# An attention and expert kernel on one core: GpSimd's place behind VectorE, and the seed of the last ranking

## The chip, the core and the metric

The kernel runs on one core of a Trainium2 chip. The metric is device time in microseconds (us) of one execution; a stated time is the median of its runs. TensorE (PE) multiplies matrices, VectorE (DVE), ScalarE (ACT) and GpSimd (POOL) work elementwise, SyncE (SP) issues transfers.

## The reference

Four batches, eight heads, 768 tokens, 64 dimensions a head: 32 heads in all. Each query and key gets a bucket from the signs of six projections, and a query attends only to keys of its own bucket. The heads' outputs are laid side by side as x, and in each batch the 128 tokens with the highest gate score go through a two-layer expert.

```python
def _attn_ref(q, k, v, proj):
    ...
    mask = q_bucket[:, :, :, None] == k_bucket[:, :, None, :]
    scores = scale * np.matmul(q, k.transpose(0, 1, 3, 2))
    scores = np.where(mask, scores, -1000000000.0)
    scores = scores - np.max(scores, axis=-1, keepdims=True)
    attn = np.exp(scores)
    attn = attn / (np.sum(attn, axis=-1, keepdims=True) + 1e-09)
    return np.matmul(attn, v)

def _moe_ref(x, w_gate, w1, w2, capacity):
    scores = np.einsum('bsd,d->bs', x, w_gate)
    out = x.copy()
    for b in range(B):
        top_idx = np.argpartition(-scores[b], capacity)[:capacity]
        xe = x[b, top_idx]
        h = np.maximum(xe @ w1, 0.0)
        ye = h @ w2
        g = 1.0 / (1.0 + np.exp(-scores[b, top_idx]))
        out[b, top_idx] = x[b, top_idx] + g[:, None] * ye
    return out
```

## The kernel before, in words

**Work and order.** The kernel cuts all its work into some 2,500 small steps (a function with its arguments), records them in a list, and then calls them in the order of a table of numbers, `ORDER`. Entry k calls step k; a negative entry resumes one of eight generators (-1 is `weights`, -2 to -4 are `choose` for batches 0 to 2, -5 is `rank_last` for the last batch). The calls run under a manual schedule, so each engine's instructions stand in the order in which the table calls them. An engine works through its own list in order and waits on semaphores only where data or buffers need it.

**A head.** For each head h and each of its six blocks of 128 queries, `max_unit` multiplies the block with the keys in two halves (L671, two of four rotating PSUM banks), `max_relu` (ACT, L679) reads the first half and frees its bank, `max_red` (DVE, L688, tile mj) combines it with the second half into a row maximum in M, and frees that bank. M is turned and written back into a row of A by way of a transfer, so that the scores come out already reduced by the maximum. `st_unit` (PE, L722 and L726) makes the transposed scores and `st_exp` (ACT, L740 and L742) their exponentials P in fp32. For a precise product, P is used as its high half (read straight out of the fp32 words) and a rest R = P minus that half. `r_chunk` makes R: for one chunk of 128 keys on DVE (L757, 128x768), or for a pair of chunks on GpSimd (L760, 128x1536). GpSimd has the middle pair in even heads and the two outer pairs in odd heads. `av` (PE, L776) multiplies P and R with V, three matmuls a block. Then `recip` and `norm` (DVE, L786 to L798) divide into x.

**Other work of the two engines.** DVE also makes low halves: of the projected inputs (L502), of V (L556), of key differences (L661) and of signs (L487), each an instruction with two inputs in SBUF. `score` (L813, tile jks) multiplies x with the gate weights and sums, also two SBUF inputs. GpSimd makes the low halves of the expert's weights (L837, 128x512) as `weights` is resumed.

**How GpSimd is ordered against DVE.** `mine(i)` remembers a DVE instruction with two SBUF inputs, the latest one in `ORDER`; `turn(i)` makes a GpSimd instruction wait by semaphore for the one remembered at that point. So which DVE instruction a GpSimd one waits for is set by where its entry stands in `ORDER`. A GpSimd instruction is free to start while later DVE instructions with two SBUF inputs run. L813 is not remembered before the change (except where another function wraps it).

**The last batch.** After the last head, `rank_last` broadcasts the scores along rows with twelve fp32 matmul passes (L1143, tiles bp) that ACT copies to sbc (L1149), DVE compares them (L859), PE counts into rp (L866), DVE turns the counts into a rank (L1167) and six `pick` instructions (L874) make a 0/1 selection out of it, which PE multiplies with x (L1177). The PSUM tiles here rotate through a pool of three buffers, which the keep-warm matmuls (L311, tile wq) take from too. Between them PE runs the expert of batch 2 (L995, L1019).

Of the kernel before, what the change touches and what calls it, by code (L numbers as in the profile page):

```python
# [20 lines left out]
P = 128  # L21
# [222 lines left out]
def body(ctx, tc, qk, v, pj, wg, w1, w2, cst, out):  # L244
# [114 lines left out]
    def mine(i):  # L359
        st["port"] = i  # L360
# [441 lines left out]
    def score(b, part, d0, d1, t0, t1):  # L802

        if ("sc", b, part) not in st:
            st["sc", b, part] = sb.tile([P, NC], F32, tag=f"sc{part}", name=f"sc{b}_{part}", bufs=1)
        need(*(("nd", b * H + d // D) for d in range(d0, d1, D)))
        x, sc = st["x", b], st["sc", b, part]
        if part:
            need(*(("scd", b, 0, t) for t in range(t0, t1)))
        for t in range(t0, t1):  # L810
            st["scd", b, part, t] = True
            jk = sb.tile([P, 384], BF16, tag="jks", name=f"jks{b}_{part}_{t}", bufs=2)
            nc.vector.tensor_tensor_reduce(  # L813
                out=jk[:, : d1 - d0], in0=x[:, t, d0:d1], in1=wgt[:, d0:d1],
                op0=ALU.mult, op1=ALU.add, scale=1.0,
                scalar=st["sc", b, part - 1][:, t : t + 1] if part else 0.0,
                accum_out=sc[:, t : t + 1],
            )
# [45 lines left out]
    def count(i, cm, rp):  # L864
        for j in range(i, NC):
            nc.tensor.matmul(  # L866
                rp[:, j : j + 1], cm[:, j], oneb[:, 0:1], start=(i == j == NC - 1), stop=(i == 0),
                skip_group_check=True,
            )
# [259 lines left out]
    def rank_last(b):  # L1129
# [23 lines left out]
        rp = st_bank(f"rp{b}")  # L1153
        yield
        cnt = sb.tile([P, NC], F32, tag="cnt", name=f"cnt{b}", bufs=1)
        cms = {}
        for i in range(NC - 1, -1, -1):
# [3 lines left out]
            if i < NC - 1:  # L1161
                count(i + 1, cms[i + 1], rp)
                yield
        count(0, cms[0], rp)
# [4 lines left out]
        for t in range(NC):  # L1169
            pick(sel, t, rank)  # L1170
# [197 lines left out]
```

## Time and profile before

| what | before |
|---|---|
| median of 3 runs | 390.51 us (390.12 to 391.72) |
| the profiled execution | 389.61 us |
| its span in the trace | 387.5 us |
| PE busy | 374.8 us, 97% |
| DVE busy | 345.9 us, 89% |
| ACT busy | 313.3 us, 81% |
| POOL busy | 181.2 us, 47% |

The span is the time from the first to the last instruction that the trace holds; 2.1 us of the execution lie around it. The profiled execution is 0.90 us below the median of the runs. Busy time of PE is the time in which at least one matmul is in flight. In the timeline a row is one or several like instructions with their start and length; a bracket behind it holds the idle time of the engine before it and what ended that.

### The profile page before, as it was taken

What the parts mean: (1) busy time and instruction counts of PE and PEld (TensorE: products, weight loads), DVE (VectorE), ACT (ScalarE), POOL (GpSimd) and SP (SyncE); (2) the same over time, 40 slices, a digit from 0 to 9 for tenths busy, and PEclk for the clock granted to TensorE, in tenths of its full rate; (3) what the DMA queues carried; (4) which work ended last, traced back from release to release, by engine and by line L of the source; (5) the groups of instructions that cost most, each with busy time, mean ns of one, the idle gap of its engine ahead of it and who ended that gap; (6) DMA issues with size and microseconds to landing.
All of it is one profiled execution on the core that took longest, in us unless ns stands there. A gap on an engine that the chain in (4) does not pass through costs nothing.

```text
span 387.5 us, 14129 instructions
## 1 busy us (share of the span) xinstructions
PE 374.8 (97%) x5728; PEld 272.6 (70%) x5738; DVE 345.9 (89%) x935; ACT 313.3 (81%) x665; POOL 181.2 (47%) x103
## 2 busy tenths in 40 slices
PE   6889999999999999999999999999999999999995
PEld 4346777677676777687657877667677788778794
DVE  3889999999899989999999999999999999999842
ACT  7899999899998988988588888988988995774210
POOL 8135567474647275655335362545236352630113
PEclk9799999999999999999999999999999999999999
DMA  7568677677776475565855552756463524010301
GB/s 243 148 193 232 172 199 232 169 203 177 223 209 181 100 214 125 140 188 150 208 136 157 135 155 61 217 161 177 100 178 103 113 58 125 6 38 3 110 29 56
DMA packets 26353, 56.37 MB, mean 145 GB/s; under 512 B 4218, under 2 KB 10942, under 8 KB 26288
## 3 DMA queue, kind: packets, MB, share of 16 engines
q1 hardware_dynamic: 15936, 36.92, 36.6%
q10 hardware_dynamic: 9680, 16.45, 13.5%
q0 software_dynamic: 672, 2.10, 1.7%
q8 instruction: 45, 0.74, 0.8%
q14 instruction: 20, 0.16, 0.2%
HBM read 26.58 MB, written 7.35 MB: 88 GB/s over the span
## 4 chain that ended last, share of the span: by engine, by line
PE 78%; issue 7%; ACT 5%; DVE 5%; DMA 2%; POOL 1%; POOLq 0%; SPq 0%; ACTq 0%; DVEq 0%
PE av L776 24%; PE bank L671 14%; PE st L722 14%; PE st L726 14%; PE bank L463 3%; PE bank L995 3%; PE bank L1019 2%; DMA A<-sg 2%; DVE R L757 2%; ACT me L679 1%; ACT P L740 1%; DMA Xa<-in_qk_dram 1%; DVE mj L688 1%; DVE jks L813 1%; PE bank L598 1%
## 5 line engine op out<-in xcount | busy, mean ns | idle before, releaser
L760 POOL TENSOR_TENSOR R<-P 128x1536 f16<-128x1536 f32 x46 | 133.8, 2910 | 134.4 <-DVE V L556 21.1
L776 PEld LDWEIGHTS <-P 128*128 128x128 bf16 x2304 | 125.8, 98 | 26.7 <-issue 1.3
L776 PE MATMUL av<-V,P 128*128 128x65 f16 (+2 forms) x2304 | 133.3, 193 | 0.1
L776 PE MATMUL av<-V,R 128*128 128x65 f16 (+1 forms) x1152 | 126.4, 193 | 0.0
L740 ACT ACTIVATE P<-st 128x512 f32<-128x512 f32 x192 | 111.9, 598 | 17.7 <-PE av L776 9.7
L722 PE MATMUL st<-A 128*128 128x512 f16 (+1 forms) x384 | 119.3, 326 | 1.4 <-ACT P L740 1.2
L726 PE MATMUL st<-B 128*128 128x512 f16 (+1 forms) x384 | 118.6, 326 | 0.7 <-ACT B L432 0.7
L688 DVE CUSTOM_DVE_ANT_0 mj<-bank,me 128x384 bf16<-128x384 f32 x192 | 102.2, 550 | 15.6 <-ACT me L679 7.4
L671 PE MATMUL bank<-A 128*128 128x384 f16 x384 | 108.4, 329 | 3.8 <-DVE A L410 1.0
L776 PEld LDWEIGHTS <-R 128*128 128x128 f16 x1152 | 105.9, 97 | 0.1
L679 ACT ACTIVATE me<-bank 128x384 f32<-128x384 f32 x192 | 92.4, 491 | 14.8 <-PE bank L671 5.7
L757 DVE TENSOR_TENSOR R<-P 128x768 f16<-128x768 f32 x100 | 96.8, 987 | 0.4 <-ACT P L740 0.2
L742 ACT ACTIVATE P<-st 128x512 f32<-128x512 f32 x96 | 56.9, 596 | 2.2 <-PE st L726 0.7
L671 PEld LDWEIGHTS <-A 128*128 128x128 f16 x384 | 34.8, 98 | 23.1 <-issue 4.8
L726 PEld LDWEIGHTS <-B 128*128 128x128 f16 x384 | 37.5, 98 | 18.0 <-issue 2.5
L722 PEld LDWEIGHTS <-A 128*128 128x128 f16 x384 | 37.4, 97 | 15.8 <-issue 2.5
L502 DVE SCALAR_TENSOR_TENSOR T<-X,T 128x768 f16<-128x768 f32 x32 | 31.4, 992 | 0.0
L495 ACT ACTIVATE T<-X 128x768 f16<-128x768 f32 x32 | 26.6, 841 | 0.4 <-DMA B<-T 0.4
L837 POOL TENSOR_TENSOR w1l<-W,w1h 128x512 bf16<-128x512 f32 x8 | 12.8, 1604 | 13.6 <-DVE M L688 4.9
L837 POOL TENSOR_TENSOR w2l<-W,w2h 128x512 bf16<-128x512 f32 x8 | 12.3, 1545 | 12.5 <-DVE R L757 4.0
L798 DVE TENSOR_TENSOR x<-av,rc 128x384 f32<-128x384 f32 x32 | 17.7, 553 | 0.2
L995 PEld LDWEIGHTS <-w1h 128*128 128x128 f16 x256 | 15.9, 98 | 2.1
(137 smaller groups left out, 409.5 us busy)
## 6 DMA issues: line engine op xcount, KB each, us to landing
X<-in_qk_dram SPq DMA_DIRECT2D x32, 384.0 KB
B<-T SPq DMA_DIRECT2D x62, 192.0 KB
A<-T SPq DMA_DIRECT2D x31, 240.0 KB
V<-in_v_dram ACTq DMA_DIRECT2D x16, 384.0 KB
out_dram<-x ACTq DMA_DIRECT2D x6, 768.0 KB
W<-in_w_dram ACTq DMA_DIRECT2D x8, 512.0 KB
sbc<-scores SPq DMA_DIRECT2D x3, 384.0 KB
A<-sg SPq DMA_DIRECT2D x31, 31.5 KB
```

The source lines that it names most:

```text
L502: mine(nc.vector.scalar_tensor_tensor(t[:, o : o + S], st["X", p, r], XS, t[:, i : i + S], op0=ALU.mult, op1=ALU.subtract))
L671: nc.tensor.matmul(pt[:, :384], a[0][:, t * P : (t + 1) * P], a[1][:, 384:768] if i else K[h % NA], start=True, stop=True,)
L679: nc.scalar.activation(me, st["mx", h, t, 0][:, :384], AF.Relu)
L688: nc.vector.tensor_tensor_reduce(out=jk, in0=st["mx", h, t, 1][:, :384], in1=st["me", h, t], op0=ALU.add, op1=ALU.max, scale=1.0 / MS, sca ...
L722: nc.tensor.matmul(pt[:, o : o + n], a[1][:, c * P : (c + 1) * P], a[0][:, q0 : q0 + n], start=True, stop=False,)
L726: nc.tensor.matmul(pt[:, o : o + n], bt[:, 0, c * P : (c + 1) * P], bt[:, 1, q0 : q0 + n], start=False, stop=True,)
L740: nc.scalar.activation(pp[:, r, 0:512], pt, AF.Exp, scale=ES)
L742: nc.scalar.activation(pp[:, :, 512:768], pt.rearrange("p (a b) -> p a b", a=2), AF.Exp, scale=ES)
L757: mine(nc.vector.tensor_tensor(t[:, r], pp[:, r], hi_view(pp, r), op=ALU.subtract))
L760: turn(nc.gpsimd.tensor_tensor(t, pp, hi_view(pp, a), op=ALU.subtract))
L776: nc.tensor.matmul(o[:, t, :n], l, vv[:, c, hh, v0 : v0 + n], start=False, stop=last and l is lo, skip_group_check=True,)
L995: nc.tensor.matmul(hp[:, f * P : (f + 1) * P], w[:, k, o : o + P], x[:, k * P : (k + 1) * P], start=(f == 0 and k == 0 and i == order[0]), ...
```

## The change

It does three things.

- `ORDER`: the entries of 34 of the 62 GpSimd instructions of L760 and L837 move some places later, behind a later DVE instruction with two SBUF inputs, which `turn` then makes them wait for. The order of the instructions on each engine stays as it was.
- `score` passes its instruction to `mine`, so that a GpSimd instruction can wait for L813 too; nine of the 34 do.
- `rank_last`: a new fp32 matmul, `behind(rp)`, puts six columns of constants into the count tile ahead of the counts, which then only add to it. The six picks of the last batch compare with one scalar (the rank) and no longer subtract a second one.

```diff
-    225, 121, -1, 239, 240, 401, 241, 132, 133, 235, -1, 224, 122, 118, 242, 226, 124, 191, 185,
+    225, 121, 239, 240, 401, 241, 132, 133, 235, -1, 224, 122, -1, 118, 242, 226, 124, 191, 185,
...
-    283, 281, 372, 389, 391, 282, 473, -1, 554, 269, 392, 285, 329, 332, 484, 477, 284, 522, 374,
-    336, 523, 278, 375, 475, 451, 465, 474, 333, 466, 467, 277, 275, 280, 276, 344, 337, 373, 749,
-    338, 746, 478, 555, 894, 342, 376, 468, 479, 286, 469, 334, 470, 476, 462, 287, 339, -1, 480,
+    283, 281, 372, 389, 391, 282, 473, 554, 269, -1, 392, 285, 329, 332, 484, 477, 284, 522, 374,
+    336, 523, 278, 375, 475, 451, 465, 474, 333, 466, 467, 277, 275, 280, 276, 337, 373, 749, 338,
+    746, 478, 555, 344, 894, 342, 376, 468, 479, 286, 469, 334, 470, 476, 462, 287, 339, -1, 480,
...
-            nc.vector.tensor_tensor_reduce(
+            mine(nc.vector.tensor_tensor_reduce(
...
-            )
+            ))
...
+    def behind(rp):
+        nc.tensor.matmul(
+            rp[:, :NC], ident, cs[:, 3 * P + NC : 3 * P + 2 * NC], start=True, stop=False, skip_group_check=True
+        )
+
-    def count(i, cm, rp):
+    def count(i, cm, rp, first=True):
...
-                rp[:, j : j + 1], cm[:, j], oneb[:, 0:1], start=(i == j == NC - 1), stop=(i == 0),
+                rp[:, j : j + 1], cm[:, j], oneb[:, 0:1], start=first and i == j == NC - 1, stop=(i == 0),
...
         rp = st_bank(f"rp{b}")
+        behind(rp)
...
-                count(i + 1, cms[i + 1], rp)
+                count(i + 1, cms[i + 1], rp, False)
...
-        count(0, cms[0], rp)
+        count(0, cms[0], rp, False)
...
         for t in range(NC):
-            pick(sel, t, rank)
+            nc.vector.tensor_scalar(sel[:, t], iota16, rank[:, t : t + 1], None, op0=ALU.is_equal)
```

In the third pair of lines entry 344 is the GpSimd rest of head 3's first pair; it moves behind entry 555, V's low half of pair 3 (L556).

GpSimd, from the first pair of head 5 to the second half of the seventh weight piece (R is the rest, P its input, w1l and w2l the weights' low halves; the numbers are buffers), before:

```order
L760 TENSOR_TENSOR R_0_1609<-P_0_1441 128x1536 [waits PE_49,Pool_49]
L760 TENSOR_TENSOR R_2_1710<-P_2_1650 128x1536 [waits DVE_49,Activation_49,Pool_49]
L837 TENSOR_TENSOR w1l<-W_1412,w1h 128x512 [waits DVE_49,Activation_49]
L760 TENSOR_TENSOR R_1_1867<-P_1_1801 128x1536 [waits DVE_49,Activation_49]
L760 TENSOR_TENSOR R_0_2085<-P_0_1949 128x1536 [waits DVE_49,Pool_49]
L837 TENSOR_TENSOR w2l<-W_2006,w2h 128x512 [waits DMAHW5_49,DVE_49,Activation_49]
L760 TENSOR_TENSOR R_2_2193<-P_2_2094 128x1536 [waits DVE_49,PE_49,Activation_49]
...
L837 TENSOR_TENSOR w2l<-W_2328,w2h 128x512
```

The same instructions with the change:

```order
L760 TENSOR_TENSOR R_0_1609<-P_0_1441 128x1536 [waits DVE_49,PE_49,Pool_49]
L760 TENSOR_TENSOR R_2_1710<-P_2_1650 128x1536 [waits DVE_49,Activation_49,Pool_49]
L837 TENSOR_TENSOR w1l<-W_1412,w1h 128x512 [waits DVE_49]
L760 TENSOR_TENSOR R_1_1873<-P_1_1800 128x1536 [waits DVE_49,Activation_49]
L760 TENSOR_TENSOR R_0_2085<-P_0_1949 128x1536 [waits DVE_49,Pool_49]
L837 TENSOR_TENSOR w2l<-W_2006,w2h 128x512 [waits DMAHW5_49,DVE_49]
L760 TENSOR_TENSOR R_2_2193<-P_2_2094 128x1536 [waits PE_49,Activation_49]
...
L837 TENSOR_TENSOR w2l<-W_2328,w2h 128x512 [waits DVE_49]
```

The instructions and their order are the same; the first row and the last have a DVE wait that they had not, the second waits for a later DVE instruction under the same semaphore, and a wait that the DVE one already covers falls away in three rows.

PE, at the start of the last ranking (bp is the broadcast, wq the keep-warm tile, rp the count tile, cm what is counted), before:

```order
L1143 MATMUL bp_1_8340<-cs,sc_2_8333 128x128 [waits DVE_49,PE_49]
L1143 MATMUL bp_1_8340<-cs,sc_2_8333 128x128 x2
L1143 MATMUL bp_0_8346<-cs,sc_2_8333 128x128 x3
L311 LDWEIGHTS ones_78
L311 MATMUL wq_8355<-ones_78 128x128
...
L1019 LDWEIGHTS hth_8221 [waits Activation_49]
...
L866 LDWEIGHTS cm_5_8353 [waits PE_49,DVE_49]
L866 MATMUL rp_8351<-oneb,cm_5_8353 128x1 [waits Activation_49]
```

With the change (lines below the new function are five or six higher):

```order
L1148 MATMUL bp_1_8340<-cs,sc_2_8333 128x128 [waits DVE_49,PE_49]
L1148 MATMUL bp_1_8340<-cs,sc_2_8333 128x128 x2
L1148 MATMUL bp_0_8346<-cs,sc_2_8333 128x128 x3
L865 MATMUL rp_8351<-cs 128x6
L311 LDWEIGHTS ones_78 [waits PE_49]
L311 MATMUL wq_8356<-ones_78 128x128 [waits Activation_49]
...
L1024 LDWEIGHTS hth_8221
...
L871 LDWEIGHTS cm_5_8354 [waits DVE_49]
L871 MATMUL rp_8351<-oneb,cm_5_8354 128x1
```

The count tile now takes its buffer ahead of the keep-warm tile, which gets the buffer of bp_1: the wait for ACT's copies of bp_1 moves from the first count to the first keep-warm matmul.

## Rows read from the trace of the kernel before

**Rows 1.** The page's span and the engines' busy time, with instructions.

```profile
span 387.5 us, 14129 instructions
...
PE 374.8 (97%) x5728; PEld 272.6 (70%) x5738; DVE 345.9 (89%) x935; ACT 313.3 (81%) x665; POOL 181.2 (47%) x103
```

**Rows 2.** Busy time by stretch, with clock, DMA share and GB/s behind it.

```profile
63.00:101.00 38.00, 37.89 (x587) 26.62 (x586) 37.29 (x95) 35.99 (x78) 22.29 (x11) 1.00 0.69 189
...
250.00:300.00 50.00, 49.14 (x766) 35.06 (x763) 47.87 (x141) 43.80 (x96) 23.27 (x9) 1.00 0.54 145
```

**Rows 3.** Timeline of DVE, heads 2 to 7: start, length, instruction, idle before.

```profile
46.33 0.95 DVE L502 SCALAR_TENSOR_TENSOR T<-X,T 128x768 f16<-128x768 f32 x1
...
54.99 0.95 DVE L556 SCALAR_TENSOR_TENSOR V<-V,V 128x768 f16<-128x768 f32 x1
...
62.52 0.56 DVE L688 CUSTOM_DVE_ANT_0 mj<-bank,me 128x384 bf16<-128x384 f32 x1 [0.46 <-PE bank L671]
...
63.00 1.02 DVE L502 SCALAR_TENSOR_TENSOR T<-X,T 128x768 f16<-128x768 f32 x1
...
83.43 1.51 DVE L757 TENSOR_TENSOR R<-P 128x768 f16<-128x768 f32 x1
...
86.69 0.36 DVE L661 TENSOR_TENSOR T<-T 128x384 f16<-128x384 f16 x1
...
101.22 0.56 DVE L688 CUSTOM_DVE_ANT_0 mj<-bank,me 128x384 bf16<-128x384 f32 x1 [0.52 <-PE bank L671]
```

**Rows 4.** Timeline of POOL, heads 2 to 6.

```profile
47.45 2.75 POOL L760 TENSOR_TENSOR R<-P 128x1536 f16<-128x1536 f32 x1 [1.37 <-DVE T L502]
...
55.24 3.31 POOL L760 TENSOR_TENSOR R<-P 128x1536 f16<-128x1536 f32 x1 [0.98 <-ACT P L740]
60.10 3.11 POOL L760 TENSOR_TENSOR R<-P 128x1536 f16<-128x1536 f32 x1 [1.56 <-ACT P L740]
63.17 1.89 POOL L837 TENSOR_TENSOR w1l<-W,w1h 128x512 bf16<-128x512 f32 x1
...
75.45 1.16 POOL L837 TENSOR_TENSOR w1l<-W,w1h 128x512 bf16<-128x512 f32 x1 [4.87 <-DVE M L688]
...
81.36 2.77 POOL L760 TENSOR_TENSOR R<-P 128x1536 f16<-128x1536 f32 x1 [1.85 <-DVE R L757]
...
86.80 2.86 POOL L760 TENSOR_TENSOR R<-P 128x1536 f16<-128x1536 f32 x1
```

**Rows 5.** The chain of waits around 82 us: start, length, what.

```profile
80.24 0.95 DVE R L757
...
82.06 0.32 PE bank L671
```

**Rows 6.** Timeline of DVE in head 29.

```profile
331.38 1.55 DVE L556 SCALAR_TENSOR_TENSOR V<-V,V 128x768 f16<-128x768 f32 x1
...
334.93 1.43 DVE L757 TENSOR_TENSOR R<-P 128x768 f16<-128x768 f32 x1
```

**Rows 7.** Timeline of PE in head 29.

```profile
336.41 0.21 PE L776 MATMUL av<-V,R 128*128 128x65 f16 x1
```

**Rows 8.** Timeline of PE in the last ranking.

```profile
361.67 1.56 PE L1143 MATMUL bp<-cs,sc 128*128 128x128 f32 x12
363.07 0.50 PE L311 MATMUL wq<-ones 128*128 128x128 f16 x6
...
368.58 0.38 PE L1019 MATMUL bank<-w2l,hth 128*128 128x512 bf16 x1
368.79 2.84 PE L1177 MATMUL bank<-sel,xs 128*128 128x128 f16 x48
```

**Rows 9.** Timeline of ACT there: the copies of bp.

```profile
362.65 1.09 ACT L1149 COPY sbc<-bp 128x128 f32<-128x128 f32 x3 [0.18 <-PE bp L1143]
```

**Rows 10.** Timeline of DVE there: the picks.

```profile
367.89 1.43 DVE L874 TENSOR_SCALAR sel<-iota,cs,rank 128x128 f16<-128x128 f16 x6
```

**Rows 11.** Groups by line and form, ACT in the stretch 362 to 364: busy, mean ns.

```profile
L1149 ACT COPY sbc<-bp 128x384 f32<-128x384 f32 x1 | 0.5, 479 | 0.1
```

76 rows, old and new, of the table ORDER are left out of this document.

## The prediction
> **What bounds the kernel now.** I read the busy times first [rows 1]. PE is busy for 374.8 of 387.5 us, so whatever does not delay PE costs nothing, and DVE with 345.9 is the only engine near it. The second view is the busy time by stretch [rows 2]. From 63 to 101 us PE is busy for 37.89 of 38.00 us and DVE for 37.29: both are full at once. From 250 to 300 DVE has 2.1 us of 50 over, and the other stretches of that length are alike. So a loss on DVE weighs most between 63 and 101.
>
> The third view is DVE's timeline [rows 3]. At 62.52 DVE had stood idle for 0.46 us, for a bank from PE, and at 101.22 for 0.52; between the two I found no bracket above 0.06. DVE has no reserve there. The chain of waits says that PE hangs on it [rows 5]: DVE's R at 80.24, two shorter DVE instructions, then PE's matmul at 82.06, which needed a bank that DVE had to free. A later DVE there makes a later PE.
>
> **What a GpSimd instruction costs, free and ordered.** A reader should look at two pairs. The rest at 47.45 waited by semaphore for the L502 that ran from 46.33 to 47.28 [rows 3, 4]. It began 0.17 us after that, took 2.75 and so ended 2.92 after DVE. The rest at 55.24 had no such wait; it began while L556 ran from 54.99 to 55.94, took 3.31, and ended at 58.55, only 2.61 after DVE [rows 3, 4]. So the instruction that starts into DVE's is held, but part of its start is behind it once DVE lets go. L556 took 0.95 there, as L502 did without a neighbour: DVE, which led, lost nothing.
>
> That is the first main step. In the 34 places DVE already went first, so a semaphore gives DVE nothing that it had not, and GpSimd ends 2.92 − 2.61 = 0.31 us later. The weights' half alone takes 1.16; the one at 63.17 ended at 65.06, which is 1.04 after the L502 of 63.00 to 64.02 [rows 3, 4]. With the same 0.17 for the semaphore it would end 1.33 after: 0.29 later, an estimate from these rows.
>
> The Trainium skill, page SBUF — State Buffer, section Two separate sides (with Who interferes with whom under it) says that DVE and GpSimd share a port pair as an exclusive lock, that whoever starts first has it for the whole instruction, and that a blocked one (there it was a descriptor write) went on about 115 ns after DVE's end. The trace agrees with the lock (3.31 against 2.75), and not with the 115 ns for this instruction: by that an unordered rest would end 0.115 + 2.75 = 2.87 after DVE, where it ended 2.61 after. By the page's figure the eight places below would lose 0.05 each, an estimate of 0.4 in all, in place of 2.2.
>
> **Part 1: 63 to 101 us.** Here DVE then loses. Its next instruction with two SBUF inputs finds GpSimd still at work and is held till it ends. The L757 at 83.43 shows it: 1.51 us where 0.95 is its length alone, held by the rest that ran from 81.36 to 84.13 [rows 3, 4]. I went through all eight moved instructions of this stretch whose end already touches a DVE one: five rests (the first at 60.10, the last at 86.80) and three weights' halves (the first at 63.17). If each ends 0.31 or 0.29 later, DVE is released as much later: 5 x 0.31 + 3 x 0.29 = 2.4. Two or three of them only graze (L661 at 86.69 took 0.36 for half the columns of an L757), so I take **2.2**. Bounds: 2.5 if every place pays 0.31, and 0 if PE's lead hides it. I choose the upper side since DVE has no idle time between the first and the last of them and PE waits for DVE in the middle [rows 3, 5]. Once PE is late it stays late: it is 97% busy [rows 1], and what it issues later, transfers included, is shifted with it.
>
> **Part 2: the other places.** 17 more of the moved ones touch a DVE instruction elsewhere. There DVE has 2 to 3 us of idle time in 50 [rows 2], and 0.3 is mostly taken up. One place speaks against that: in head 29 L556 ran late to 332.93 [rows 6], the rest behind it held L757 at 334.93 for 1.43 us, and PE's first product with that R came at 336.41, right at its end of 336.36 [rows 6, 7]. That is 0.3 on PE. In a second place, head 11, I count 0.1. Together **0.4**; bounds 0 and 1.5 (five such places).
>
> **Part 3: the last ranking.** Six fp32 columns are added on PE. The trace has no such matmul; twelve passes of 128 columns took 1.56 us [rows 8], so two passes of six columns lie between nothing and 0.26 us; nearest in passes is 0.1. But the keep-warm matmuls behind it now wait for ACT's first two copies of bp. Three copies took 1.09 from 362.65, to 363.74, and the third alone takes 0.48 [rows 9, 11], so the second ends at about 363.26; before, the keep-warm matmuls began at 363.07 [rows 8]. The new matmul lies inside that wait. PE goes on **0.2** later (0.05 to 0.3), and from there it is contiguous to the end. Keep-warm matmuls themselves are no work that anyone waits for, but the expert's are queued behind them.
>
> The picks take 1.43 us for six [rows 10]. The first product with them began at 368.79 right behind the expert's matmul of 368.58, one pitch of 0.21 later [rows 8], and the first pick was ready at about 367.89 + 1.43 / 6 = 368.13. One scalar fewer on DVE shortens nothing that PE waits for: **0**; bound below 0.3, should later picks be what sets the pace of the 48 products. If that cover went, half of 1.43 would be the most to gain or lose.
>
> **The sum.** 2.2 + 0.4 + 0.2 = 2.8 on the profiled execution: 389.61 + 2.8 = 392.4. The median of the runs stood 0.90 above that execution; on it the sum gives 390.51 + 2.8 = **393.3 us**, with 391.8 to 395.0 for this case alone (half of part 1 at one end; all upper bounds, 4.3, with a little scatter at the other).
>
> **Rivals.**
>
> *PE's lead hides it (16%).* The max stage has four banks, and DVE idles at 62.52 and 101.22 for a bank from PE [rows 3]. If PE's own pace decides there, the delay fills those gaps and only the last ranking and head 29 are left: 390.51 + 0.5 = 391.0. Against it speak the PE wait at 82.06 [rows 5] and the sum of the gaps, 1.0 against 2.2.
>
> *The hand-over is short (6%).* If an unordered instruction gains only 0.05 by starting early, part 1 is 0.4 and part 2 nothing: 391.1. That is the skill page's figure, named above; the 2.61 against 2.92 speaks against it in every rest that I looked at.
>
> *The ordering takes collisions away (18%), the other side.* One mechanism: who gets the pair. A rest ordered behind DVE starts 0.17 after it. Where DVE's next instruction has two SBUF inputs too, that one takes the pair in this gap, runs free, and GpSimd comes behind both. Today the eight held instructions lose 1.6 us together (0.56 at 83.43). In other executions GpSimd may also win where the lead is short (0.11 between 86.69 and 86.80 [rows 3, 4]), and hold DVE for up to 2.75; the median's 0.90 above the profile bounds what that costs typically. If all of it goes, 390.51 − 1.6 − 0.9 + 0.2 = 388.2; half of it gives 389.5. It decides from the point where PE follows DVE in that stretch. Against it: behind each of the eight the next DVE instruction takes an input from PSUM (L688, once L786), so GpSimd should start as planned.
>
> *It does not do what it says (6%).* The new waits are fulfilled long before they are reached, since GpSimd waits for P or a buffer anyway. Then only part 3 is left: 390.7. Against it: the held rests show that they reached DVE's instruction while it ran.
>
> **How the numbers follow.** The forecast has 54%. Half a percent, about what a measurement of this kernel can tell from no change, is 1.95 us: 388.56 to 392.46. Some 9 of the 54 points lie under 392.46, so slower has 0.45. Faster is the greater part of the third rival, 0.11. No change has the rest: 9 + 16 + 6 + 6 + 7 = 0.44. The range leaves out the far end of the third rival (some 13 points) and 3 points above: 388.9 to 395.0.
>
> **What would show it.** Right: the moved rests of L760 take 2.75 alone, with a bracket for DVE ahead of them, and end 2.9 after DVE; the held L757 instructions of 63 to 101 take longer than 1.43 to 1.51; PE reaches the matmul of 82.06 some 1.4 later, the end of the stretch 2 later, and the first keep-warm matmul stands behind ACT's second copy. Wrong: if the stretch up to 101 is no longer, part 1 is; if held L757 instructions are as short as 0.95, the third rival holds; if L760 still takes 3.1 to 3.5, the waits are idle. The last products begin behind the expert's matmul as before, or part 3's zero is wrong.

## The result and the profile after

| what | before | after |
|---|---|---|
| median | 390.40 us (389.79 to 391.72, 6 runs) | 395.39 us (394.96 to 396.35, 6 runs) |
| ratio of after to before | | 1.0127, 95% interval 1.0106 to 1.0147 |
| span of the profiled execution | 387.5 us | 393.1 us |

The change costs 5.0 us. The forecast had the side and named the mechanism, but said 2.8 us; the time lies 0.4 us above its range. The page after, answering to [rows 1], and the shares of the chain that ended last, before and then after:

```profile
span 393.1 us, 14144 instructions
...
PE 378.8 (96%) x5740; PEld 273.5 (70%) x5740; DVE 353.3 (90%) x935; ACT 314.7 (80%) x665; POOL 169.0 (43%) x103
```

```profile
PE 78%; issue 7%; ACT 5%; DVE 5%; DMA 2%; POOL 1%; POOLq 0%; SPq 0%; ACTq 0%; DVEq 0%
```

```profile
PE 67%; DVE 14%; issue 8%; ACT 6%; POOL 2%; DMA 1%; POOLq 0%; SPq 0%; DVEq 0%; ACTq 0%
```

GpSimd is busy for 12 us less, DVE for 7.4 us more, and DVE's share of the last chain rises from 5% to 14%. That is the signature of the change: GpSimd no longer stands inside its instructions and waits for DVE, but DVE stands inside its own and waits for GpSimd. The groups by line and form show it, GpSimd's rests before and after and then DVE's rests before and after (busy us, mean ns, idle before):

```profile
L760 POOL TENSOR_TENSOR R<-P 128x1536 f16<-128x1536 f32 x46 | 133.8, 2910 | 134.4 <-DVE V L556 21.1 <-DVE R L757 20.3 <-ACT me L679 12.6
...
L757 DVE TENSOR_TENSOR R<-P 128x768 f16<-128x768 f32 x100 | 96.8, 987 | 0.4 <-ACT P L740 0.2
```

```profile
L760 POOL TENSOR_TENSOR R<-P 128x1536 f16<-128x1536 f32 x46 | 126.9, 2758 | 143.1 <-DVE V L556 21.2 <-DVE rc L786 20.3 <-DVE R L757 20.3
...
L757 DVE TENSOR_TENSOR R<-P 128x768 f16<-128x768 f32 x100 | 101.2, 1031 | 0.5 <-ACT P L742 0.2 <-ACT P L740 0.2
```

A single place, in the timelines of POOL and then of DVE after the change, beside [rows 3, 4]:

```profile
56.27 2.75 POOL L760 TENSOR_TENSOR R<-P 128x1536 f16<-128x1536 f32 x1 [1.85 <-DVE V L556]
...
83.28 2.75 POOL L760 TENSOR_TENSOR R<-P 128x1536 f16<-128x1536 f32 x1 [2.19 <-DVE sc L813]
```

```profile
55.15 0.94 DVE L556 SCALAR_TENSOR_TENSOR V<-V,V 128x768 f16<-128x768 f32 x1
...
63.12 1.31 DVE L502 SCALAR_TENSOR_TENSOR T<-X,T 128x768 f16<-128x768 f32 x1
...
82.69 0.41 DVE L813 CUSTOM_DVE_ANT_0 jks<-x,wgt 128x256 bf16<-128x256 f32 x1
...
85.01 1.83 DVE L757 TENSOR_TENSOR R<-P 128x768 f16<-128x768 f32 x1
...
103.62 0.56 DVE L688 CUSTOM_DVE_ANT_0 mj<-bank,me 128x384 bf16<-128x384 f32 x1 [0.52 <-PE bank L671]
```

The rest at 56.27 took 2.75 where it had taken 3.31, began 0.18 after the end of L556 at 56.09, and ended at 59.02, 2.93 after it; before, it had ended 2.61 after. The L502 at 63.12 is held for 1.31 (1.02 before), the L757 at 85.01 for 1.83 (1.51 before). All eight places of the stretch are longer by 0.2 to 0.35 like these.

**Where the 5 us lie.** DVE's instructions stand in the same order in both traces, so each one's start can be set against its own start before. The difference was 0.11 us at the L688 that starts at 61.60 after the change, 2.40 at the L688 of 103.62 (101.22 before), 5.13 when PE begins the last ranking (366.80, 361.67 before), and 5.31 when it begins the last products (374.10, 368.79 before). So the stretch to 101 lost 2.29, the stretch from 101 to the last ranking 2.73, and the ranking 0.18. One more held place lies ahead of the first stretch: the L502 that took 0.96 at 54.10 before takes 1.24; the 0.11 is what was left of this and of an earlier start. Busy time by stretch, after (and, in the second fence, the middle stretch of before):

```profile
63.00:103.40 40.40, 38.98 (x588) 26.79 (x587) 39.69 (x95) 36.52 (x79) 19.71 (x11) 1.00 0.65 180
103.40:365.50 262.10, 260.00 (x4161) 190.42 (x4160) 249.44 (x674) 216.33 (x460) 111.23 (x48) 1.00 0.48 132
```

```profile
101.00:360.40 259.40, 257.21 (x4154) 190.19 (x4161) 244.13 (x674) 215.60 (x461) 118.46 (x48) 1.00 0.49 134
```

In the first stretch PE now idles for 1.42 us, where it had idled for 0.11. Its longest waits there are these, one for DVE's row maxima and one for GpSimd's rest itself (a second one for a rest, at 92.12, is 0.17 long):

```profile
69.46 0.85 PE L463 MATMUL bank<-X,pjt 128*32 128x384 f32 x8 [0.60 <-DVE M L688]
...
81.14 0.20 PE L776 MATMUL av<-V,R 128*128 128x65 f16 x1 [0.43 <-POOL R L760]
```

A rest that ends later so delays PE by two roads, through the DVE instruction that it holds and by its own result. By 101 PE is as late as DVE: its matmul that started at 100.75 before starts at 103.14, 2.4 later.

In the middle DVE is busy for 5.31 us more, of which 2.73 reached the end. PE's idle time there is the same (2.19 before, 2.10 after); its loss shows as 2.79 us more of busy time with the same work, since a matmul in flight counts as busy.

PE in the last ranking after the change, and DVE's picks:

```profile
366.80 1.56 PE L1148 MATMUL bp<-cs,sc 128*128 128x128 f32 x12
368.20 0.28 PE L865 MATMUL rp<-cs 128*128 128x6 f32 x2
368.37 0.49 PE L311 MATMUL wq<-ones 128*128 128x128 f16 x6
...
373.88 0.38 PE L1024 MATMUL bank<-w2l,hth 128*128 128x512 bf16 x1
374.10 2.84 PE L1183 MATMUL bank<-sel,xs 128*128 128x128 f16 x48
```

```profile
373.19 1.07 DVE L1176 TENSOR_SCALAR sel<-iota,rank 128x128 f16<-128x128 f16 x6
```

The keep-warm matmuls begin 1.57 after the broadcast (1.40 before [rows 8]), 0.17 later. The picks fell from 1.43 to 1.07 us for six [rows 10], and the products still begin one pitch behind the expert's last matmul: nothing won.

### The profile page after: what moved, and what is told of

Same layout as the page of the kernel before. It is cut to its first block, busy times and chain, and to the rows that moved or that the text cites. A ratio compares the mean times of both kernels' runs of the same rounds, so it can differ in the third digit from the quotient of the medians.

```text
span 393.1 us, 14144 instructions
## 1 busy us (share of the span) xinstructions
PE 378.8 (96%) x5740; PEld 273.5 (70%) x5740; DVE 353.3 (90%) x935; ACT 314.7 (80%) x665; POOL 169.0 (43%) x103
## 4 chain that ended last, share of the span: by engine, by line
PE 67%; DVE 14%; issue 8%; ACT 6%; POOL 2%; DMA 1%; POOLq 0%; SPq 0%; DVEq 0%; ACTq 0%
PE av L776 21%; PE bank L671 13%; PE st L722 12%; PE st L726 12%; DVE R L757 5%; DVE mj L688 3%; PE bank L1000 3%; PE bank L1024 2%; PE bank L463 2%; ACT me L679 2%; DVE jks L813 1%; DVE T L502 1%; ACT P L740 1%; DMA Xa<-in_qk_dram 1%; POOL R L760 1%
## 5 line engine op out<-in xcount | busy, mean ns | idle before, releaser
L760 POOL TENSOR_TENSOR R<-P 128x1536 f16<-128x1536 f32 x46 | 126.9, 2758 | 143.1 <-DVE V L556 21.2
L688 DVE CUSTOM_DVE_ANT_0 mj<-bank,me 128x384 bf16<-128x384 f32 x192 | 102.0, 549 | 14.1 <-ACT me L679 6.9
L757 DVE TENSOR_TENSOR R<-P 128x768 f16<-128x768 f32 x100 | 101.2, 1031 | 0.5 <-ACT P L742 0.2
L502 DVE SCALAR_TENSOR_TENSOR T<-X,T 128x768 f16<-128x768 f32 x32 | 32.6, 1030 | 0.0
L837 POOL TENSOR_TENSOR w1l<-W,w1h 128x512 bf16<-128x512 f32 x8 | 9.8, 1224 | 17.9 <-DVE R L757 7.3
L837 POOL TENSOR_TENSOR w2l<-W,w2h 128x512 bf16<-128x512 f32 x8 | 9.9, 1233 | 16.6 <-DVE R L757 8.8
```

Source lines behind the costliest of these rows:

```text
L502: mine(nc.vector.scalar_tensor_tensor(t[:, o : o + S], st["X", p, r], XS, t[:, i : i + S], op0=ALU.mult, op1=ALU.subtract))
L688: nc.vector.tensor_tensor_reduce(out=jk, in0=st["mx", h, t, 1][:, :384], in1=st["me", h, t], op0=ALU.add, op1=ALU.max, scale=1.0 / MS, sca ...
L757: mine(nc.vector.tensor_tensor(t[:, r], pp[:, r], hi_view(pp, r), op=ALU.subtract))
L760: turn(nc.gpsimd.tensor_tensor(t, pp, hi_view(pp, a), op=ALU.subtract))
```

## The experiments

All were built from the changed kernel. "Moved" are the 34 places; where a moved wait is undone, the instruction keeps its place in the program and waits for the DVE instruction that it waited for before:

```diff
+            n = st["turns"] = st.get("turns", -1) + 1
+            dep = st["ports"][OLD[n]] if n in OLD else st["port"]
             tc.add_manual_dep(
-                getattr(i, "ins", i), getattr(st["port"], "ins", st["port"]).name,
+                getattr(i, "ins", i), getattr(dep, "ins", dep).name,
```

The kernel before ran on the same chip each time; its median is given with each group. Two experiments have one run each.

### Which part costs: waits, last ranking, first places, later places

The first takes the last ranking back:

```diff
-        behind(rp)
...
-                count(i + 1, cms[i + 1], rp, False)
+                count(i + 1, cms[i + 1], rp)
...
-            nc.vector.tensor_scalar(sel[:, t], iota16, rank[:, t : t + 1], None, op0=ALU.is_equal)
+            pick(sel, t, rank)
```

> The changed order and the scores' waits alone; the last ranking and its picks as before. Theory A (each moved GpSimd instruction ends 0.31 us later behind DVE and holds DVE's next one as much longer; the last ranking adds 0.18): 4.8 over the kernel before, about 395.2. Rival B (the last ranking and the picks bring a large part): under 394.

The second undoes all 34 waits (`OLD` names them all) and keeps the ranking.

> The seed matmul and the one-scalar picks alone; all of GpSimd's waits as before. Theory A: the first keep-warm matmul starts some 0.18 later, so 390.6, no change that can be told. Rival B: over 391.5.

The third and the fourth take the ranking back and undo the later 22 or the first twelve.

> Only the moved waits of the first twelve places (up to 101 us of the kernel before); the others wait for what they waited for before, the last ranking as before. Theory A: DVE is 2.4 us late at 101 us and nothing more is added, so about 392.8. Rival C (lateness of the first part grows later by itself, since transfers and other engines then meet differently): over 394.

> Only the moved waits of the later 22 places; the first twelve wait as before, the last ranking as before. Theory A: no difference up to 101 us, then about 2.7 more, about 393.0. Rival C: DVE's idle time takes nearly all of it, under 391.2.

| kernel | median | ratio to before (389.83 us) | interval |
|---|---|---|---|
| waits only | 395.23 | 1.0126 | 1.0110 to 1.0143 |
| ranking only | 390.08 | 1.0006 | 0.9994 to 1.0018 |
| first twelve waits | 392.19 | 1.0052 | 1.0038 to 1.0065 |
| later 22 waits | 392.14 | 1.0052 | 1.0038 to 1.0065 |

Rival B is out: the ranking is not to be told from no change, and the waits carry the loss. Rival C is out on both counts: the first places cost 2.4 and do not grow, the later ones cost 2.3 with nothing late ahead of them. But both halves lie under what theory A gave them, by 0.6 and 0.9. They sum to 4.7, both together measured 5.4; some 0.7 comes only when they meet, or lies in the spread of the runs.

### Is it the late end, or any start by semaphore?

A small wrapper remembers each DVE instruction that is written; `mine` keeps the one just ahead of the leader (the DVE instruction that a GpSimd one is to stand behind), and GpSimd waits for that:

```diff
+            def call(*a, **kw):
+                Vec.prev, Vec.last = Vec.last, f(*a, **kw)
+                return Vec.last
...
     def mine(i):
-        st["port"] = i
+        st["port"] = Vec.prev or i
```

> The changed order without the change to the last ranking; each of the 62 GpSimd instructions waits for the DVE instruction just ahead of the one that it is to stand behind, not for that one itself. Theory A (what costs is that an ordered GpSimd instruction starts only after its DVE leader has ended, and then ends 2.92 behind it in place of 2.61): it now starts while its leader runs, ends about 2.61 after it in all 62 places, the 34 lose nothing and the other 28 gain 0.31 where they hold a DVE instruction: 387 to 389.5, below the kernel before (389.8). Rival D (a start by semaphore costs as such): 394 to 395.5. Rival E (a leader that itself waits for data lets GpSimd take the pair first, and is held up to 2.75): over 391.

Measured: 390.66 us, 1.0016 of the kernel before (390.14), interval 1.0002 to 1.0029. A semaphore at every place, and 0.5 of the 5.4 us is left: rival D falls, and the late end is the cause. GpSimd's rests in that kernel, by line and form (its lines are 14 higher, and all its DVE instructions carry the wrapper's line):

```profile
L774 POOL TENSOR_TENSOR R<-P 128x1536 f16<-128x1536 f32 x46 | 138.0, 3000 | 129.2 <-DVE V L254 26.2 <-ACT P L754 24.6 <-DVE R L254 15.7
```

They stand inside DVE's instructions again (3000 ns). But the kernel is not below the one before, as theory A had it. Its DVE timeline shows two reasons (the second fence has the rest at 104.03 as it was in the kernel before):

```profile
28.59 2.78 DVE L254 TENSOR_TENSOR R<-P 128x768 f16<-128x768 f32 x2
...
104.03 0.97 DVE L254 TENSOR_TENSOR R<-P 128x768 f16<-128x768 f32 x1
105.65 0.56 DVE L254 CUSTOM_DVE_ANT_0 mj<-bank,me 128x384 bf16<-128x384 f32 x1 [0.38 <-ACT me L693]
...
170.10 1.92 DVE L254 SCALAR_TENSOR_TENSOR T<-X,T 128x768 f16<-128x768 f32 x1
```

```profile
103.36 1.39 DVE L757 TENSOR_TENSOR R<-P 128x768 f16<-128x768 f32 x1
```

At 28.59 (the second of the two) and 170.10 an earlier weights' half holds a DVE instruction for 1.9 us that took 0.95 before. And at 104.03 a rest on DVE is 0.42 shorter than before (0.97 against 1.39), but two instructions later DVE idles for 0.38 that it had not: what DVE gains, PE and ACT do not follow.

Two more of this kind. Without any wait at all (`TURNS = False`):

> The same without any of the waits that order GpSimd behind DVE, in any of the 62 places; last ranking as before. Theory A: the 62 places lose no hand-over, but in those where GpSimd's data are there first it starts ahead of a DVE instruction of 0.95 and holds it for up to 2.75. The 28 places where the kernel before has an effective wait are these; if a third of them hold DVE for 1 us more: 391 to 400. Rival F (the waits are of no use): 387 to 389.5, as with the wait one instruction ahead.

Measured: 447.75 us, ratio 1.1471 (1.1442 to 1.1499), far beyond either. Its page and the group of DVE's rests:

```profile
PE 388.2 (87%) x5728; PEld 277.3 (62%) x5738; DVE 400.1 (90%) x935; ACT 315.3 (71%) x665; POOL 181.2 (41%) x103
...
L757 DVE TENSOR_TENSOR R<-P 128x768 f16<-128x768 f32 x100 | 120.2, 1220 | 0.5 <-ACT P L740 0.2
```

L757 takes 1220 ns on average where 987 was the mean before, and DVE is busy for 400.1 us. GpSimd now takes the pair first and holds DVE. Who goes first is worth 57 us; the change, which moves waits to a later instruction, won nothing of this, since in its 34 places DVE went first already.

With the 34 as before and only the other 28 waiting one instruction ahead:

> The 34 moved places wait for what they waited for in the kernel before (they run unordered behind their leader), the other 28 for the DVE instruction just ahead of their leader; last ranking as before. Theory A: the 28 end 0.31 earlier behind their leader; DVE gains that where they hold its next instruction, in about half of the places, and some is lost to idle time: 1 to 4 us under the kernel before, 386 to 389. Rival D: 389.8, as before. Rival E: over 390.5.

Measured: 391.16 us, 1.0037 (1.0019 to 1.0056): rival E. At least four instructions of DVE were held by some 0.6 to 1 us more (by the same two weights' halves and two others), against gains that turned into idle time.

### Only where DVE is held?

Ten of the moved waits, whose GpSimd instruction held no DVE instruction in the trace after, and then the other 24:

> Of the 34 moved waits only the ten whose GpSimd instruction, in the trace of the changed kernel, ends without holding a DVE instruction by more than 0.1 us; the other 24 as in the kernel before, last ranking as before. Theory A (a later end costs only through a held DVE instruction): no change, within 0.5 us of the kernel before. Rival H (every ordered place costs its 0.3, through R being late for PE or through the queue): 1.5 to 3 us slower.

> The counterpart: the 24 moved waits whose GpSimd instruction holds a DVE instruction; the ten others and the last ranking as before. Theory A: the whole loss, 4.6 to 5.2 us over the kernel before. Rival H: 24 of 34 parts of it, about 3.4.

Measured beside 390.20: 390.78 (1.0014, 1.0000 to 1.0027) and 395.39 (1.0142, 1.0121 to 1.0162). The 24 carry the whole loss, so rival H is out. Within the 24 the two roads to PE, a held DVE instruction and a late rest, were not parted. The ten cost 0.6, a little over the expected 0.5; in their trace three instructions of DVE are held by 0.2 to 0.4 more. The first is held by a rest that stands in GpSimd's queue behind a moved weights' half; a place is quiet only if what is queued behind it is quiet too. The other two take back what DVE had won at a gap, as the last experiment shows.

### A version that takes back the early weights' halves

As the kernel with all waits one ahead, but two places wait for their leader:

```diff
+            n = st["turns"] = st.get("turns", -1) + 1
+            dep = st["lead"] if n in PLAIN else st["port"]
```

> As the kernel in which each GpSimd instruction waits for the DVE instruction ahead of its leader (390.66), but two weights' halves (the third and the thirty-eighth step of the weights) wait for the leader itself again: their early start had held DVE for 0.97 and 0.65 us more. Theory A: these 1.6 us come back, 389.0 to 389.6, just below the kernel before (390.1). Rival G (PE sets the end there too and DVE's gain turns into idle time): 390.1 to 390.7.

Measured: 389.49 us against 390.20, 0.9988 (0.9976 to 0.9999): just below the kernel before, and 5.9 under the changed one by the medians. Its page:

```profile
PE 375.3 (97%) x5738; PEld 272.8 (70%) x5738; DVE 341.8 (88%) x935; ACT 313.4 (81%) x665; POOL 184.3 (48%) x103
```

DVE is busy for 4.1 us less than before and the time fell by 0.7. Theory A's time is met, and rival G holds a part: most of DVE's gain turned into idle time.

### One place by itself

In head 8 the rest behind L813 held an L757 for 1.77 us after the change and 1.03 before: 0.74, more than the price of one place. Two experiments, with one and with three moved waits:

> One moved wait alone: the middle rest of head 8, behind L813; all else as in the kernel before. Looked at: the L757 that it holds (1.03 us in the kernel before, 1.77 in the changed one). Carried lateness (GpSimd's end moves by 0.31 of its own, and by whatever DVE was late when it was released, though DVE itself makes that up in its idle gap of 0.34 between): here nothing is late before it, so 1.34. Rival I (0.74 is this place's own price): 1.7 to 1.8.

> The same wait and the two moved weights' halves ahead of it (heads 7 and 8), which hold two L757 ahead of the gap by 0.22 each. Carried lateness: DVE is 0.44 late before its gap and 0.0 to 0.1 behind it, but the rest is released 0.44 later, so the L757 takes 1.34 + 0.35 to 0.44 = 1.7 to 1.8. Rival J (the gap takes up what lies before it): 1.34.

DVE's timeline with one moved wait (lines four higher), the place itself and the next gap:

```profile
109.56 1.45 DVE L761 TENSOR_TENSOR R<-P 128x768 f16<-128x768 f32 x1
...
120.98 0.49 DVE L491 TENSOR_TENSOR sg<-sg 128x384 f16<-128x384 f16 x1
121.49 0.56 DVE L692 CUSTOM_DVE_ANT_0 mj<-bank,me 128x384 bf16<-128x384 f32 x1
...
123.81 1.39 DVE L506 SCALAR_TENSOR_TENSOR T<-X,T 128x768 f16<-128x768 f32 x1
```

The same three behind the place in the kernel before, and a rest on POOL, first of before and then of the experiment:

```profile
120.59 0.49 DVE L487 TENSOR_TENSOR sg<-sg 128x384 f16<-128x384 f16 x1
121.33 0.56 DVE L688 CUSTOM_DVE_ANT_0 mj<-bank,me 128x384 bf16<-128x384 f32 x1 [0.25 <-PE bank L671]
...
123.66 1.15 DVE L502 SCALAR_TENSOR_TENSOR T<-X,T 128x768 f16<-128x768 f32 x1
...
121.25 2.75 POOL L760 TENSOR_TENSOR R<-P 128x1536 f16<-128x1536 f32 x1 [0.38 <-DVE sg L487]
```

```profile
121.64 2.75 POOL L764 TENSOR_TENSOR R<-P 128x1536 f16<-128x1536 f32 x1 [0.39 <-ACT WH L611]
```

Alone the L757 is held for 0.42 more (1.45 against 1.03; 1.34 was expected), so 0.74 is not the place's own price, and rival I is out. And a little later the carrying is to be seen. DVE is 0.39 late at 120.98. Its gap of 0.25 takes most of that up, and at 121.49 it is only 0.16 late. But the rest was released ahead of the gap and is 0.39 late still (121.64 against 121.25), and its end holds the next DVE instruction with two SBUF inputs for 1.39 where it was 1.15: DVE is 0.39 late again. An idle gap of DVE does not help what GpSimd carries past it.

With three moved waits the L757 was not held, which neither reading had:

```profile
106.70 1.65 DVE L761 TENSOR_TENSOR R<-P 128x768 f16<-128x768 f32 x1
108.27 0.41 DVE L817 CUSTOM_DVE_ANT_0 jks<-x,wgt 128x256 bf16<-128x256 f32 x1
...
109.38 0.16 DVE L790 TENSOR_SCALAR rc<-av 128x6 f32<-128x6 f32 x1 [0.68 <-PE av L780]
...
111.42 1.00 DVE L761 TENSOR_TENSOR R<-P 128x768 f16<-128x768 f32 x1
```

The two waits ahead held DVE (1.65 against 1.44 at the second), but the gap in front of L790 did not take that up; it grew from 0.33 to 0.68, since PE's av came later still, and the L761 behind it was not held at all.

What the 0.74 is made of can be read from the traces of the other runs. The gap in front of L786 differs from trace to trace, also where no wait was moved, so the length of the L757 by itself is no measure of the place. The time from the start of L813 to the end of the held L757 is one. The kernel before, the changed one and the run with the ranking alone:

```profile
106.79 0.41 DVE L813 CUSTOM_DVE_ANT_0 jks<-x,wgt 128x256 bf16<-128x256 f32 x1
...
107.54 0.17 DVE L786 TENSOR_SCALAR rc<-av 128x6 f32<-128x6 f32 x1 [0.33 <-PE av L776]
...
109.59 1.03 DVE L757 TENSOR_TENSOR R<-P 128x768 f16<-128x768 f32 x1
```

```profile
109.61 0.41 DVE L813 CUSTOM_DVE_ANT_0 jks<-x,wgt 128x256 bf16<-128x256 f32 x1
...
111.99 1.77 DVE L757 TENSOR_TENSOR R<-P 128x768 f16<-128x768 f32 x1
```

```profile
106.38 0.41 DVE L817 CUSTOM_DVE_ANT_0 jks<-x,wgt 128x256 bf16<-128x256 f32 x1
...
108.89 1.32 DVE L761 TENSOR_TENSOR R<-P 128x768 f16<-128x768 f32 x1
```

| trace | wait of this rest | gap before L786 | held L757 | from L813's start to L757's end |
|---|---|---|---|---|
| before | as before | 0.33 | 1.03 | 3.83 |
| ranking only | as before | under 0.05 | 1.32 | 3.83 |
| first twelve waits | as before | under 0.05 | 1.45 | 3.84 |
| changed kernel | behind L813 | under 0.05 | 1.77 | 4.15 |
| later 22 waits | behind L813 | 0.20 | 1.48 | 4.15 |
| one moved wait | behind L813 | 0.23 | 1.45 | 4.15 |
| three moved waits | behind L813 | 0.68 | 1.00 | 4.15 |

So the place costs 0.32 in every trace, whatever stands around it. The rest is released ahead of the gap, and its end sets the end of the held L757; a shorter gap makes the L757 start sooner and take longer. Of the 0.74 in the changed kernel 0.32 is the price, and 0.42 is what DVE had won at the gap and lost again; of the 0.42 with one moved wait it is 0.32 and 0.10.

The times were 389.76 and 391.19 us beside one run of 389.68; single runs, and the second one's DVE was 1.05 us later already at 103, ahead of the places.

## Why the prediction was right or wrong

- **DVE went first already, so the wait gives nothing and costs GpSimd 0.31.** Right. The rests take 2758 ns in place of 2910 and end 2.93 after DVE at the place shown; with the wait one instruction ahead, which leaves the late end out, 0.5 of the 5.4 us is left. At the place of head 8 the price is 0.32 in each of the four traces that the table of the last experiment has.
- **The Trainium skill's 115 ns.** The Trainium skill's page SBUF — State Buffer (section Two separate sides) has the lock as exclusive, and the traces agree: GpSimd's moved rests are held no more, and in its place DVE is. By its 115 ns part 1 would have been 0.4; it is 2.29. The rival *the hand-over is short*, 391.1, is out at 395.39.
- **Part 1, 63 to 101 us: 2.2.** Right: 2.29 in the trace, 2.4 from the run with the first twelve waits alone (392.19 against 389.83). PE idled there for 1.42 us against 0.11, for DVE and for GpSimd's rests, and reached the matmul of 82.06 at 83.64, 1.58 later.
- **Part 2, the other places: 0.4, at most 1.5.** This is the step that failed, a term mis-sized nearly seven times: 2.73 in the trace, 2.3 from the run with the later 22 alone, and outside its own bounds. The text said that DVE "has 2 to 3 us of idle time in 50 [rows 2], and 0.3 is mostly taken up". DVE was busy for 5.31 us more there and only about half of it was taken up: its idle time fell by 2.61, from 15.27 to 12.66 of the stretch. The idle time was counted as reserve without asking what ends it and where it lies. Some gaps stay: the one at 101.22 waits for a bank from PE, and after the change it is still 0.52 at 103.62, since PE had become as late as DVE, and with 2.19 us idle in 259.40 it had little to catch up with. Others shrink in vain: four, at 107.54, 121.33, 183.18 and 186.22 of the kernel before, lie between the release of a rest and the DVE instruction that it holds. They gave up some 1.4 of the 2.61, and the holds behind them grew by about as much. So three places cost 0.74, 0.51 and 0.69 in place of 0.31. The last of them, before and after:

```profile
186.22 0.56 DVE L688 CUSTOM_DVE_ANT_0 mj<-bank,me 128x384 bf16<-128x384 f32 x1 [0.52 <-PE bank L671]
...
187.19 0.96 DVE L757 TENSOR_TENSOR R<-P 128x768 f16<-128x768 f32 x1
```

```profile
190.38 0.56 DVE L688 CUSTOM_DVE_ANT_0 mj<-bank,me 128x384 bf16<-128x384 f32 x1
...
191.34 1.65 DVE L757 TENSOR_TENSOR R<-P 128x768 f16<-128x768 f32 x1
```

This account of the gaps is read from the traces; no run was made to change a gap alone. At the place of head 8 the trace of the ranking alone has that case: the gap fell from 0.33 to under 0.05, no wait was moved, and the hold grew from 1.03 to 1.32. The place at 54.10, held for 0.28 more, belongs to this part too and is not in the 2.73.
- **Part 3, the ranking: 0.2.** Right: 0.18 in the trace; alone 1.0006 with 1 inside the interval. The picks are worth 0, as said. The reason given for the 0.2 was the wait for ACT's copies; the new matmul alone, from 368.20 to the keep-warm one at 368.37, is as long. The keep-warm one begins 0.05 after ACT's second copy has ended (367.78 + 0.54 = 368.32), which speaks for the wait, but no run tells the two apart. In the kernel before that copy ended at 363.19 (362.65 + 0.54), not at the 363.26 of the prediction; with the same 0.05 the wait alone gives 0.17.
- **PE's lead hides it** fell with PE's idle time in the first stretch. **The ordering takes collisions away** fell: none of DVE's held instructions in the first stretch became shorter. **It does not do what it says** fell with the 2758 ns.

What was forecast for a single place held, 0.2 to 0.35 wherever no gap of DVE stood between; the error was a sum over many of them under one sentence on idle time.

## What to carry to other kernels

When instructions of two engines hold each other up and one already goes first, a wait on the leader costs the hand-over each time and gives nothing. A wait on the instruction just ahead of the leader lets the follower queue inside the leader; it kept the order here in all but a few places, which are to be looked for in the trace. No wait at all lost 57 us, so which places need one is the first question. Idle time of an engine is a reserve only for what does not delay the engine it waits for, and never where it lies between the release of another engine's instruction and the one that this holds: ask of each gap what ends it and what runs across it. And the two directions are not alike: 7.4 us more on DVE cost 5.0, 4.1 us less gained 0.7. The traces put this down to PE, which was right behind; no run made PE faster to test it.

## What the runs showed of the hardware

A GpSimd rest (128x1536) that starts inside a DVE instruction of two SBUF inputs ends 2.61 us after it (21 of the 22 such rests in the kernel before lie at 2.60 to 2.61), though it takes 2.75 alone: by these numbers some 0.14 us of it is done before DVE lets go, an estimate. One that is released by DVE's semaphore starts 0.14 to 0.18 after DVE's end and so ends 2.89 to 2.93 after it (41 rests after the change). The two together are 0.28 to 0.32. For a weights' half (128x512) the two ends are 1.01 to 1.03 and 1.23 to 1.31. The other way round, a DVE rest (128x768, 0.95 alone) that runs into GpSimd's ends 0.81 after it: the L757 of 85.01 ends at 86.84, GpSimd's rest of 83.28 at 86.03. It was also not expected that all the waits together decide over 57 us of 390.
